# A chunked-attention and expert-routing kernel: first loads by casting DMA, routing matmuls placed later, another order of the last chain

## The chip, the cores and the metric

The kernel runs on one core of one Trainium2 chip. The metric is the device time of one execution in microseconds (us). The time before is the median of three runs, 166.93 us (166.66 to 167.89). A profile is of another single execution: its span, from the first to the last instruction, is 161.9 us, and that execution's time 163.59 us.

The engines are named as in the profile: PE (TensorE; its weight loads are PEld), DVE (VectorE), ACT (ScalarE), POOL (GpSimd), SP (SyncE). [...]

## The reference

Two layers, one after the other. Attention in chunks of 32 queries, each over 8 memory rows, 16 rows to the left, the chunk and 8 rows to the right; batch 4, 8 heads, 768 positions, head size 64:

```python
for c in range(nc):                              # nc = 768 // 32
    k_ctx = k[:, :, l_start:r_end]               # up to 56 rows
    k_full = np.concatenate([mem_k, k_ctx], axis=2)
    v_full = np.concatenate([mem_v, v_ctx], axis=2)
    scores = scale * np.matmul(q_c, k_full.transpose(0, 1, 3, 2))
    a = np.exp(scores - max); a = a / (sum + 1e-09)
    out[:, :, c_start:c_end] = np.matmul(a, v_full)
```

Then, for each batch, a gate score for each of the 768 rows x of 512 numbers; the 128 rows with the highest score go through a feed-forward net (FFN, 512 to 1024 to 512), and its output, weighted by the sigmoid of the score, is added to the row:

```python
scores = np.einsum('bsd,d->bs', x, w_gate)
for b in range(B):
    top_idx = np.argpartition(-scores[b], capacity)[:capacity]    # capacity = 128
    xe = x[b, top_idx]
    ye = np.maximum(xe @ w1, 0.0) @ w2
    g = 1.0 / (1.0 + np.exp(-scores[b, top_idx]))
    out[b, top_idx] = x[b, top_idx] + g[:, None] * ye
```

## The kernel before

The attention takes two heads (a pair) at a time: 4 pairs in a batch, 16 in all (n = 0 to 15). In each, q, k and v are transposed by PE, the scores are formed in two halves, exponentiated by ACT into `es`, and multiplied with v. The loads for two pairs (`load_unit`) are one DMA for each of k, q, v and cast fp32 to fp16 on the way; only the very first pair is loaded as fp32 and cast by DVE and ACT.

```python
def load_unit(u):
    for src, dst, nm in ((k, k16s, "k16"), (q, q16s, "q16"), (v, v16s, "v16")):
        t = ld.tile([96, 4, 512], F16, tag=nm, ...)
        dst[2 * u], dst[2 * u + 1] = t[:, 0:2, :], t[:, 2:4, :]
        if u:  nc.gpsimd.dma_start(out=t, in_=head_ap(src, 2 * u, 4))
        else:  nc.gpsimd.dma_start(out=dst[1], in_=head_ap(src, 1, 2))
for src, nm, eng in ((k, "k", nc.sync), (q, "q", nc.scalar), (v, "v", nc.sync)):
    first[nm] = cst.tile([96, 2, 512], FP, ...)
    eng.dma_start(out=first[nm], in_=head_ap(src, 0, 2))
# ... cut: constants, memory rows, units 1 to 3
```

`fill(n)` issues n matmuls of zeros (128x512) whose result nobody uses; they keep PE occupied. Before the loop:

```python
nc.vector.tensor_copy(out=k16s[0], in_=first["k"])
nc.scalar.copy(out=q16s[0], in_=first["q"])
nc.vector.tensor_copy(out=v16s[0], in_=first["v"])
fill(11); tr_k(0); tr_q(0); fill(4)
mem_rows(memk16, memkT); mem_cols(kws[0], memkT, 0)
fill(3); tr_v(0); scores(0, 0)
mem_rows(memv16, memvT)
for n in range(3): mem_cols(vws[n], memvT, n)
fill(4); tr_k(1); fill(4); scores(0, 1); tr_q(1)
fill(3); back_v(0); tr_v(1); fill(2)
late_constants()
```

The loop works ahead: pass n forms the scores of pair n+1, the values of pair n, and transposes pair n+2. Between its stages stand eight hooks, numbered i to i+7, into which the routing of an earlier batch is put:

```python
for n in range(NPR):                     # NPR = 16
    b, pr = divmod(n, NP); i = 8 * n
    nf = 0 if n in (2 * NP, 3 * NP) else 1
    if b >= 1 and pr == 0: m_store(b - 1)        # writes the batch's x to HBM
    # ... cut: at n == 14, m_alloc(LAST), m_x16(LAST, first half)
    scores(n + 1, 0, nf if b == 0 else 0); hook(i)
    tr_q(n + 2);                           hook(i + 1)
    values(n, 0, nf);                      hook(i + 2)
    tr_k(n + 2);                           hook(i + 3)
    scores(n + 1, 1, nf);                  hook(i + 4)
    back_v(n + 1)
    # ... cut: at n == 14, m_dot(LAST, first half of the columns, scrA)
    hook(i + 5)
    values(n, 1, nf);                      hook(i + 6)
    tr_v(n + 2);                           hook(i + 7)
    # ... cut: load_unit, load_w
```

The routing of batch b begins at hook 32(b+1). Its steps and their places (`at(place, step)`):

```python
dots, cmps, counts = (0, 3, 6, 7, 8, 11), (15, 16, 19, 22, 23, 24), (17, 18, 20, 23, 24, 25)
row0, row1, gate, sel, fetch = 9, 13, 14, 26, 29
# b == LAST - 1: dots (0,1,3,4,6,7), cmps (11,12,14,15,16,17), counts (12,14,15,16,17,18),
#                row0, row1, gate, sel, fetch = 7, 9, 13, 19, 20
# m_dot:   DVE, gate score of 128 rows           -> scr
# m_row:   PE transposes of scr (fp32), ACT copy -> brow (all scores on every partition)
# m_cmp:   DVE, brow < scr                       -> gr
# m_count: PE, 6 matmuls gr x ones               -> p_c (how many score higher)
# m_mask:  DVE, count < 128, running sum         -> mask, incl
# m_slot:  PE, 1 matmul; DVE                     -> slot
# m_sel:   DVE, 6 comparisons with iota          -> sel
# m_fetch: PE sel x aux -> DVE idx, gate; POOL gathers the rows xe from HBM by idx
if b < LAST - 1:
    at(33, m_rows)        # PE transposes xe, ACT copy -> xeT
    at(35, m_ffn1, 0)     # PE 16 matmuls, ACT ReLU -> hT
    at(37, m_ffn1, 1)
    at(39, m_ffn2)        # PE 8 matmuls, ACT -> y; POOL adds y to the rows in HBM
```

All these steps of batches 0 to 2 share one PSUM buffer, `pmm` (tile p_m, p_e, p_f in the profile); those of the last batch use the two buffers of the scores (p_l). After the loop:

```python
b = LAST
m_store(b)
m_dot(b, range(NB), 2, 4, scrB)
nc.vector.tensor_tensor(out=mods[b].scr, in0=scrA, in1=scrB, op=ALU.add)
fill(4)
m_row(b, 0, 4); m_gate_exp(b); m_row(b, 4, 6, "dve")
m_rows(b - 1); fill(3)
m_cmp(b, range(NB)); m_x16(b, 0, 6, 2, 4)
m_ffn1(b - 1, 0); m_count(b, range(0, 3))
m_ffn1(b - 1, 1); m_count(b, range(3, 6))
m_mask(b); m_slot(b); m_ffn2(b - 1)
m_sel(b); m_gate(b); m_gather(b); m_aux(b)
m_ffn1(b, 0); m_ffn1(b, 1); m_ffn2(b)
```

Of the kernel before, what the change touches and what calls it, by code (L numbers as in the profile page):

```python
# [17 lines left out]
def _dap(x, offset, dims):  # L18
    return bass.AP(tensor=x.tensor, offset=offset, ap=[list(d) for d in dims])
# [7 lines left out]
def kernel(  # L27
# [13 lines left out]
    nc = tc.nc  # L41
# [32 lines left out]
    def head_ap(src, n, heads):  # L74
        b, pr = divmod(n, NP)
        return _dap(src, (b * H + 2 * pr) * HD, [[512, 96], [HD, heads], [1, 512]])

    def load_unit(u):
        for src, dst, nm in ((k, k16s, "k16"), (q, q16s, "q16"), (v, v16s, "v16")):
            t = ld.tile([96, 4, 512], F16, tag=nm, name=f"{nm}_{u}")  # L80
            dst[2 * u], dst[2 * u + 1] = t[:, 0:2, :], t[:, 2:4, :]
            if u:
                nc.gpsimd.dma_start(out=t, in_=head_ap(src, 2 * u, 4))
            else:
                nc.gpsimd.dma_start(out=dst[1], in_=head_ap(src, 1, 2))


    first = {}
    for src, nm, eng in ((k, "k", nc.sync), (q, "q", nc.scalar), (v, "v", nc.sync)):
        first[nm] = cst.tile([96, 2, 512], FP, tag=f"{nm}f", name=f"{nm}f")  # L90
        eng.dma_start(out=first[nm], in_=head_ap(src, 0, 2))


    prow = cst.tile([128, 1], I32, tag="prow")
    nc.gpsimd.iota(prow, pattern=[[0, 1]], base=0, channel_multiplier=1)
    memk16 = cst.tile([B * H, n_mem * D], F16, tag="memk16")
    memv16 = cst.tile([B * H, n_mem * D], F16, tag="memv16")
    nc.gpsimd.dma_start(out=memk16, in_=_dap(mem_k, 0, [[n_mem * D, B * H], [1, n_mem * D]]))
    ident16 = cst.tile([128, 128], F16, tag="ident16")
    nc.gpsimd.memset(ident16, 1.0)  # L100
    nc.gpsimd.affine_select(out=ident16, in_=ident16, pattern=[[1, 128]], compare_op=ALU.is_equal, fill=0.0,
                            base=0, channel_multiplier=-1)
    nc.gpsimd.dma_start(out=memv16, in_=_dap(mem_v, 0, [[n_mem * D, B * H], [1, n_mem * D]]))
    for u in range(4):
        load_unit(u)


# [9 lines left out]
    def fill(n):  # L117
        fill_into(pmm.tile([128, 1, 512], FP, tag="pm", name="p_f")[:, 0, :], n)
# [3 lines left out]
    nc.vector.memset(pads[:, :, 0:1], 0.0)  # L122
    nc.vector.memset(pads[:, :, 49:50], 0.0)
    wgb = cst.tile([128, Dm], FP, tag="wgb")
    nc.sync.dma_start(out=wgb, in_=_dap(moe_w_gate, 0, [[0, 128], [1, Dm]]))

    pi = cst.tile([128, 1], I32, tag="pi")
    nc.vector.tensor_scalar(out=pi, in0=prow, scalar1=15, scalar2=None, op0=ALU.bitwise_and)
# [24 lines left out]
        vws.append(cst.tile([128, NG, 128], F16, tag=f"vw{i}", name=f"vw{i}"))  # L153
        nc.vector.tensor_copy(out=vcs[i][:, :, :, 64], in_=ones8[:, :].unsqueeze(2).to_broadcast([128, NG, 2]))

    memkT = cst.tile([128, NPR, n_mem], F16, tag="memkT")
    memvT = cst.tile([128, NPR, n_mem], F16, tag="memvT")

    def mem_rows(src, dst):
        p_mk = pmm.tile([128, n_mem, B * H], F16, tag="pm", name="p_mk")  # L160
        for j in range(n_mem):
            for hh in range(2):
                nc.tensor.transpose(out=p_mk[64 * hh:64 * hh + 64, j, :], in_=src[:, D * j:D * j + D],
                                    identity=ident16[0:B * H, 0:B * H])
        for hh in range(2):
            nc.vector.tensor_copy(out=dst[64 * hh:64 * hh + 64, :, :].rearrange("p n j -> p j n"),  # L166
                                  in_=p_mk[64 * hh:64 * hh + 64, :, hh::2])


# [43 lines left out]
    def tr_q(n):  # L213
        if n >= NPR:
            return
        p_q = pvv.tile([128, 8, 128], F16, tag="pv", name="p_q")[:, :, 0:96]
        transposes(q16s, n, p_q)
        qT = att.tile([128, 96, 8], F16, tag="qT", name="qT")
        nc.scalar.copy(out=qT, in_=p_q.rearrange("p j t -> p t j"))  # L219
        qTs[n] = qT  # L220

    def mem_cols(t, src, n):
        eng = nc.vector if n < 4 else nc.gpsimd
        eng.tensor_copy(out=t.rearrange("p g (j t) -> p g j t", t=16)[:, :, :, 15],  # L224
                              in_=src[:, n:n + 1, :].to_broadcast([128, NG, n_mem]))

    def tr_k(n):
        if n >= NPR:
            return
        transposes(k16s, n)  # L230
        kw = kws[n % SLOTS]
        nc.vector.tensor_copy(out=kw.rearrange("p g (j t) -> p g j t", t=16),  # L232
                              in_=_sap(p_t, 0, [[12, NG], [100, 8], [1, 16]]))
        if n:
            mem_cols(kw, memkT, n)

    def tr_v(n):
        if n >= NPR:
            return
        transposes(v16s, n)  # L240
        vw = vws[n % SLOTS]
        nc.scalar.copy(out=vw.rearrange("p g (j t) -> p g j t", t=16)[:, :, :, 0:15],  # L242
                       in_=_sap(p_t, 0, [[12, NG], [100, 8], [1, 15]]))
# [71 lines left out]
    def m_store(b):  # L315
        x = xs[b]
        nc.sync.dma_start(out=_dap(out, b * S * Dm, [[Dm, 96], [96 * Dm, NB], [1, Dm]]), in_=x[0:96, :, :])
        nc.sync.dma_start(out=_dap(out, (b * S + 576) * Dm, [[Dm, 32], [32 * Dm, NB], [1, Dm]]), in_=x[96:128, :, :])
# [17 lines left out]
    def m_x16(b, lo, hi, pr0=0, pr1=NP):  # L336
        c0, c1 = 2 * D * pr0, 2 * D * pr1
        nc.scalar.copy(out=mods[b].x16[:, lo:hi, c0:c1], in_=xs[b][:, lo:hi, c0:c1])
# [128 lines left out]
    def moe_steps(b):  # L467

        st = {}

        def at(i, f, *a):
            st.setdefault(i, []).append(lambda: f(b, *a))

        at(0, m_alloc)
        dots, cmps, counts = (0, 3, 6, 7, 8, 11), (15, 16, 19, 22, 23, 24), (17, 18, 20, 23, 24, 25)
        row0, row1, gate, sel, fetch = 9, 13, 14, 26, 29
        if b == LAST - 1:
            dots, cmps, counts = (0, 1, 3, 4, 6, 7), (11, 12, 14, 15, 16, 17), (12, 14, 15, 16, 17, 18)
            row0, row1, gate, sel, fetch = 7, 9, 13, 19, 20
        for i in range(NB):  # L480
            at(dots[i], m_dot, (i,))
        at(row0, m_row, 0, 4)
        at(row1, m_row, 4, 6)
        at(row1, m_gate_exp)
        at(gate, m_gate)
        for i in range(NB):
            at(cmps[i], m_cmp, (i,))
        for i in range(NB):
            at(counts[i], m_count, (i,))
        at(counts[NB - 1], m_mask)  # L490
        at(sel, m_slot)
        at(sel, m_sel)
        at(fetch, m_fetch)
        if b < LAST - 1:
            at(33, m_rows)
            at(35, m_ffn1, 0)
            at(37, m_ffn1, 1)
            at(39, m_ffn2)
        return st


# [6 lines left out]
        for f in places.get(i, ()):  # L508
            f()

    nc.vector.tensor_copy(out=k16s[0], in_=first["k"])  # L511
    nc.scalar.copy(out=q16s[0], in_=first["q"])
    nc.vector.tensor_copy(out=v16s[0], in_=first["v"])
    fill(11)
    tr_k(0)
    tr_q(0)
    fill(4)
    mem_rows(memk16, memkT)
    mem_cols(kws[0], memkT, 0)
    fill(3)  # L520
    tr_v(0)
    scores(0, 0)
    mem_rows(memv16, memvT)
    for n in range(3):
        mem_cols(vws[n], memvT, n)
    fill(4)
    tr_k(1)
    fill(4)
    scores(0, 1)
    tr_q(1)  # L530
    fill(3)
    back_v(0)
    tr_v(1)
    fill(2)
    late_constants()
    scrA = mod.tile([128, NB], FP, tag="scrA", name="scrA")
    scrB = mod.tile([128, NB], FP, tag="scrB", name="scrB")
    for n in range(NPR):
        b, pr = divmod(n, NP)
        i = 8 * n  # L540
        nf = 0 if n in (2 * NP, 3 * NP) else 1
        if b >= 1 and pr == 0:
            m_store(b - 1)
        if n == NPR - 2:
            m_alloc(LAST)
            m_x16(LAST, 0, NB, 0, 2)
        scores(n + 1, 0, nf if b == 0 else 0)
        hook(i)
        if 3 <= n + 3 < NPR:
            mem_cols(vws[(n + 3) % SLOTS], memvT, n + 3)  # L550
        tr_q(n + 2)
        hook(i + 1)
        values(n, 0, nf)
        hook(i + 2)
        tr_k(n + 2)
        hook(i + 3)
        scores(n + 1, 1, nf)
        hook(i + 4)
        back_v(n + 1)
        if n == NPR - 2:  # L560
            m_dot(LAST, range(NB), 0, 2, scrA)
        hook(i + 5)
        values(n, 1, nf)
        hook(i + 6)
        tr_v(n + 2)
        hook(i + 7)
        if n % 2 == 1 and n // 2 + 4 < NPR // 2:
            load_unit(n // 2 + 4)
        if n in (0, 2, 4, 6):
            load_w(n)  # L570
            load_w(n + 1)
# [3 lines left out]
    m_store(b)  # L575
    m_dot(b, range(NB), 2, 4, scrB)
    nc.vector.tensor_tensor(out=mods[b].scr, in0=scrA, in1=scrB, op=ALU.add)
    fill(4)
    m_row(b, 0, 4)
    m_gate_exp(b)  # L580
    m_row(b, 4, 6, "dve")
    m_rows(b - 1)
    fill(3)
    m_cmp(b, range(NB))
    m_x16(b, 0, 6, 2, 4)
    m_ffn1(b - 1, 0)
    m_count(b, range(0, 3))
    m_ffn1(b - 1, 1)
    m_count(b, range(3, 6))
    m_mask(b)  # L590
    m_slot(b)
    m_ffn2(b - 1)
    m_sel(b)
    m_gate(b)
    m_gather(b)
# [39 lines left out]
```

## Time and profile before

| | busy us | share of the span |
|---|---|---|
| PE matmuls | 131.6 | 81% |
| PE weight loads | 94.3 | 58% |
| DVE | 91.8 | 57% |
| ACT | 82.2 | 51% |
| POOL | 47.2 | 29% |
| granted PE clock, mean | 0.801 | |
| DMA, mean | 127 GB/s | |

The page has a busy row for each engine over 40 slices of the span, with the granted PE clock (PEclk) and the DMA beside them in tenths. Waits are put down to the instruction or DMA that ended them; "p_m L381 <- DVE gr L371" reads: a matmul of line 381 waited for DVE's result gr of line 371. In the whole span such waits of PE come to 6.4 us for gr, 3.2 us for the gathered rows xe, and 1.5 and 1.6 us for the copied memory rows.

### The profile page before, as it was taken

The numbers are of one execution on the slowest core, as the hardware profiler recorded it, in microseconds if no ns is written. First come the engines' busy times: TensorE is split into PE (matmuls) and PEld (weight loads), VectorE is DVE, ScalarE is ACT, GpSimd is POOL, SyncE is SP. The second block draws the span as 40 slices with busy tenths as digits, with TensorE's granted clock in tenths as the row PEclk, the third lists the DMA queues.
The fourth block names the chain that finished last, engine by engine and source line by source line (L and its number), as shares of the span: only waits on it lengthen the run. The fifth ranks groups of instructions, "written<-read, shape, count | busy, mean of one in ns | idle before, by whom it ended". The sixth has DMA issues, their size and how long they took to land. (4 is left out here: it accounts for less than half of the span.)

```text
span 161.9 us, 4777 instructions
## 1 busy us (share of the span) xinstructions
PE 131.6 (81%) x2047; PEld 94.3 (58%) x2047; DVE 91.8 (57%) x282; ACT 82.2 (51%) x160; POOL 47.2 (29%) x79
## 2 busy tenths in 40 slices
PE   6866989999999788969997889959876798688900
PEld 2332457777776666758775667848465573476500
DVE  5455227755897855835658575736469579555000
ACT  3314267898886627261777533465586220543310
POOL 7886142013675250182052200402230020002130
PEclk9995699999999955555999655687999555599996
DMA  4999999998799999059993000194050022910532
GB/s 150 249 205 207 205 206 209 205 187 140 73 217 290 253 207 200 12 111 223 247 146 59 0 4 0 11 285 135 0 65 4 0 34 71 280 42 0 69 29 36
DMA packets 15781, 20.49 MB, mean 127 GB/s; under 512 B 848, under 2 KB 10960, under 8 KB 15760
## 3 DMA queue, kind: packets, MB, share of 16 engines
q0 software_dynamic: 11792, 12.45, 49.1%
q1 hardware_dynamic: 3760, 7.34, 15.3%
q10 hardware_dynamic: 208, 0.39, 0.8%
q8 instruction: 16, 0.26, 0.6%
q14 instruction: 5, 0.04, 0.1%
HBM read 24.25 MB, written 7.34 MB: 195 GB/s over the span
## 5 line engine op out<-in xcount | busy, mean ns | idle before, releaser
L271 ACT ACTIVATE es<-p_s,maskb 128x256 f16<-128x256 f32 x96 | 38.5, 474 | 20.5 <-PE p_s L266 20.4
L292 PEld LDWEIGHTS <-es 128*32 128x32 f16 (+1 forms) x384 | 25.3, 127 | 5.6 <-issue 2.2
L292 PE MATMUL p_w<-vc,es 128*32 128x65 f16 (+1 forms) x384 | 27.2, 220 | 0.0
L242 ACT COPY vw<-p_t 128x960 f16<-128x960 f16 x16 | 15.4, 961 | 20.8 <-PE p_t L210 20.8
L224 POOL COPY kw<-memkT 128x64 f16<-128x64 f16 x12 | 8.4, 703 | 54.0 <-DVE kw L232 54.0
L295 DVE RECIPROCAL rd<-p_w 128x6 f32<-128x6 f32 x32 | 6.2, 195 | 29.1 <-PE p_w L292 28.7
L115 PE MATMUL p_f<-zeros 128*128 128x512 f16 x38 | 14.7, 535 | 5.1 <-DVE memvT L166 1.6
L296 DVE TENSOR_TENSOR x<-p_w,rd 128x384 f32<-128x384 f32 x32 | 17.8, 557 | 1.1
L251 DVE COPY vc<-p_v 128x1024 f16<-128x1024 f16 x16 | 11.1, 691 | 9.9 <-PE p_v L250 9.7
L333 DVE SCALAR_TENSOR_TENSOR junk<-x,wgb 128x512 f32<-128x512 f32 (+1 forms) x30 | 16.2, 581 | 0.0
L464 POOL DMA_INDIRECT out_dram<-y,idx x4 | 6.5, 1617 | 33.1 <-ACT y L463 27.3
L115 PEld LDWEIGHTS <-zeros 128*128 128x128 f16 x83 | 8.8, 114 | 12.4 <-issue 5.2
L371 DVE TENSOR_SCALAR gr<-brow,scr 128x768 f16<-128x768 f32 x24 | 13.7, 622 | 0.1
L219 ACT COPY qT<-p_q 128x768 f16<-128x768 f16 x16 | 13.0, 813 | 0.6 <-PE p_q L210 0.6
L115 PE MATMUL p_w<-zeros 128*128 128x512 f16 x28 | 12.9, 462 | 0.0
L266 PE MATMUL p_s<-qT,kw 64*128 64x96 f16 x256 | 12.7, 228 | 0.0
L250 PE MATMUL p_v<-ident,vw 128*128 128x128 f16 x128 | 11.9, 247 | 1.0 <-ACT qT L219 1.0
L232 DVE COPY kw<-p_t 128x1024 f16<-128x1024 f16 x16 | 11.0, 685 | 2.6 <-PE p_t L210 2.2
L266 PEld LDWEIGHTS <-kw 64*128 64x128 f16 x256 | 7.4, 104 | 7.3 <-issue 6.3
L381 PE MATMUL p_m<-onec,gr 128*128 128x1 f16 x108 | 5.6, 167 | 6.4 <-DVE gr L371 6.4
L210 PE MATMUL p_t<-ident,k 96*64 96x96 f16 x256 | 10.1, 232 | 0.7 <-DVE k L511 0.7
L250 PEld LDWEIGHTS <-vw 128*128 128x128 f16 x128 | 9.0, 110 | 2.4 <-issue 1.2
(114 smaller groups left out, 185.0 us busy)
## 6 DMA issues: line engine op xcount, KB each, us to landing
out_dram<-x SPq DMA_DIRECT2D x4, 1152.0 KB, 7.7
k<-in_k_dram POOLq DMA_DIRECT2D x7, 384.0 KB, 11.2
q<-in_q_dram POOLq DMA_DIRECT2D x7, 384.0 KB, 12.4
v<-in_v_dram POOLq DMA_DIRECT2D x7, 384.0 KB, 13.4
w_sb<-in_moe_w_dram POOLq DMA_DIRECT2D x8, 256.0 KB, 9.6
out_dram<-x SPq DMA_DIRECT2D x4, 384.0 KB, 9.1
qf<-in_q_dram ACTq DMA_DIRECT2D x1, 384.0 KB, 5.1
kf<-in_k_dram SPq DMA_DIRECT2D x1, 384.0 KB, 4.7
```

Source lines behind the costliest of these rows:

```text
L115: nc.tensor.matmul(out=ap, lhsT=zeros[:, 0:128], rhs=zeros, start=True, stop=True)
L219: nc.scalar.copy(out=qT, in_=p_q.rearrange("p j t -> p t j"))
L232: nc.vector.tensor_copy(out=kw.rearrange("p g (j t) -> p g j t", t=16), in_=_sap(p_t, 0, [[12, NG], [100, 8], [1, 16]]))
L242: nc.scalar.copy(out=vw.rearrange("p g (j t) -> p g j t", t=16)[:, :, :, 0:15], in_=_sap(p_t, 0, [[12, NG], [100, 8], [1, 15]]))
L250: nc.tensor.transpose(out=p_v[:, g, :, :], in_=vws[n % SLOTS][:, g, :], identity=ident16)
L251: nc.vector.tensor_copy(out=vcs[n % SLOTS][:, :, :, 0:64], in_=p_v)
L266: nc.tensor.matmul(out=p_s[:, h, 96 * gi:96 * gi + 96], lhsT=kw[o:o + 64, g, :], rhs=qf[o:o + 64, 96 * g:96 * g + 96], start=True, stop=True)
L271: nc.scalar.activation(out=es[:, :, :, 32 * c:32 * c + 32], in_=pv[:, :, :, 32 * c:32 * c + 32], func=AF.Exp, bias=maskb[:, c:c + 1], scal ...
L292: nc.tensor.matmul(out=p_x[r0:r1, i, h, :], lhsT=es[:, h, gi, q0:q1], rhs=vc[:, GROUPS[half][gi], h, 0:65], start=True, stop=True)
L296: nc.vector.tensor_tensor(out=xs[b].rearrange("p g (n h d) -> p n g h d", n=NP, d=D)[:, pr, 3 * half:3 * half + 3], in0=p_x[:, :, :, 0:64] ...
L333: nc.vector.scalar_tensor_tensor(out=junk[:, c0:c1], in0=x[:, bl, c0:c1], scalar=1.0, in1=wgb[:, c0:c1], op0=ALU.mult, op1=ALU.mult, accum ...
L371: nc.vector.tensor_scalar(out=m.gr[:, bl, :], in0=m.brow, scalar1=m.scr[:, bl:bl + 1], scalar2=None, op0=ALU.is_lt)
```

## The change

It does four things. The first pair's k, q and v are loaded by the casting DMA of POOL too, in the order in which they are needed, so that the casts on DVE and ACT and the fp32 buffers go; the load of the gate weights stands in pass 1. The transposed memory rows are stored in the order in which PE leaves them, so their copy writes without a stride. The routing steps get other places: those of PE stand at least two hooks behind the vector work that they need, and the FFN of batches 0 and 1 comes later. And in the last chain the rows of batch 2 and both halves of its first FFN layer stand ahead of the last batch's row transposes, the counts are one block, and some fills move. Core of the diff (cuts marked):

```diff
+    def load_half(src, dst, n):
+        nc.gpsimd.dma_start(out=dst[n], in_=head_ap(src, n, 2))
+    load_unit(0)            # now only allocates
+    load_half(k, k16s, 0)
     nc.gpsimd.iota(prow, ...)
-    # first[nm]: fp32 loads on sync and scalar, casts on DVE and ACT
+    load_half(q, q16s, 0)
+    # ... cut: ident16, load of memk16
+    load_half(v, v16s, 0)
+    # ... cut: load of memv16
+    for src, dst in ((k, k16s), (q, q16s), (v, v16s)):
+        load_half(src, dst, 1)
-    nc.sync.dma_start(out=wgb, in_=...w_gate...)     # at the start
+        if n == 1:                                    # in the loop
+            nc.sync.dma_start(out=wgb, in_=...w_gate...)
-    memkT = cst.tile([128, NPR, n_mem], ...)          # memvT alike
+    memkT = cst.tile([128, n_mem, NPR], ...)
-        nc.vector.tensor_copy(out=dst[...].rearrange("p n j -> p j n"), in_=p_mk[..., hh::2])
+        nc.vector.tensor_copy(out=dst[...], in_=p_mk[..., hh::2])
```

```diff
+        p = dict(dots=(0, 3, 6, 7, 8, 11), row0=12, row1=15, gate=17, cmps=(18, 19, 22, 23, 24, 27),
+                 counts=(22, 23, 26, 27, 28, 31), mask=32, slot=34, sel=35, fetch=38, rows=45, ffn=(47, 49, 51))
+        if b == LAST - 2:
+            p.update(fetch=37, rows=43, ffn=(45, 46, 47))
         if b == LAST - 1:
+            p = dict(dots=(0, 1, 3, 4, 6, 7), row0=9, row1=11, gate=12, cmps=(13, 14, 15, 17, 18, 19),
+                     counts=(16, 17, 18, 20, 21, 22), mask=22, slot=24, sel=24, fetch=26)
```

```diff
-    fill(11)
+    fill(8)
     tr_k(0)
+    fill(2)
     tr_q(0)
-    fill(4)
     # ... cut: likewise 3 -> 2, 0 -> 1, 4 -> 0, 4 -> 2, 3 -> 2, 2 -> 1
-        nf = 0 if n in (2 * NP, 3 * NP) else 1
+        nf = 1
     # ... cut: at n == 14 m_x16(LAST) after the second half of the scores; scrA's m_dot from n == 14 to n == 15
-    fill(4)
+    m_rows(b - 1)
+    m_ffn1(b - 1, 0)
+    m_ffn1(b - 1, 1)
     m_row(b, 0, 4)
     m_gate_exp(b)
     m_row(b, 4, 6, "dve")
-    m_rows(b - 1)
-    fill(3)
     m_cmp(b, range(NB))
+    m_ffn2(b - 1)
     m_x16(b, 0, 6, 2, 4)
-    m_ffn1(b - 1, 0)
-    m_count(b, range(0, 3))
-    m_ffn1(b - 1, 1)
-    m_count(b, range(3, 6))
+    m_count(b, range(NB))
     m_mask(b)
     m_slot(b)
-    m_ffn2(b - 1)
+    fill(3)
     m_sel(b)
```

## The prediction

> **What bounds the kernel now.** I read the page's slices first, then busy time by stage, then TensorE's (PE's) timeline inside the stages where the clock is low. Two rows of the slices (40 slices of 4.05 us) belong side by side:
>
> ```profile
> PE   6866989999999788969997889959876798688900
> PEclk9995699999999955555999655687999555599996
> ```
>
> PE is busy nearly everywhere, yet in 16 slices it was granted under 0.7 of its clock. Cut at the main loop's borders (a pass of the loop starts with the scores of the next pair of heads), the stages are: start, passes 0 to 4, passes 5 to 11, passes 12 and 13, and the rest.
>
> ```profile
> core 0: us, PE busy (x) PEld busy (x) DVE busy (x) ACT busy (x) POOL busy (x), PEclk, DMA share, GB/s
> 0.00:22.54 22.54, 16.57 (x184) 7.88 (x184) 10.08 (x41) 7.62 (x13) 13.39 (x32) 0.85 1.08 203
> 22.54:46.23 23.69, 23.51 (x500) 17.77 (x498) 15.40 (x41) 19.50 (x40) 8.35 (x16) 1.00 1.05 167
> 46.23:104.37 58.14, 51.68 (x840) 39.74 (x836) 37.08 (x105) 32.16 (x66) 17.54 (x27) 0.71 0.66 132
> 104.37:124.46 20.09, 15.35 (x268) 11.85 (x266) 12.14 (x33) 12.71 (x25) 3.71 (x4) 0.92 0.42 100
> 124.46:161.90 37.44, 24.51 (x270) 17.09 (x267) 17.06 (x70) 10.17 (x18) 4.17 (x3) 0.73 0.29 61
> ```
>
> Columns: stage, length, busy time per engine, granted clock, DMA share, GB/s. Passes 0 to 4 are the healthy state: 4.74 us each, PE full, clock 1.00. Passes 5 to 11 are PE-bound too (51.68 of 58.14 us) but at clock 0.71. Why it falls is in PE's timeline (start, length, group, idle before it and its releaser):
>
> ```profile
> 87.86 0.18 PE L378 MATMUL p_m<-zero,ltri 128*128 128x6 f16 x1
> 88.86 0.30 PE L381 MATMUL p_m<-onec,gr 128*128 128x1 f16 x6 [0.82 <-DVE gr L371]
> 89.03 0.38 PE L115 MATMUL p_w<-zeros 128*128 128x512 f16 x1
> ...
> 107.02 0.40 PE L417 MATMUL p_e<-ident,xe 128*128 128x128 f16 x4 [1.85 <-DMA xe<-out_dram,idx]
> ```
>
> PE stands in order at a routing matmul whose comparison VectorE (DVE) has just begun. Soon after each such gap the same 16 transposes take 0.85 us instead of 0.53. Asked in 1 us steps, the clock falls near 56.5, 90.6, 107.7 and 124.7 and returns near 76.9, 104.3, 111.1 and 141.8: all about whole multiples of 3.41 us apart. The gaps just before the falls are 0.88, 0.82, 1.85 and 1.27 us; gaps of 0.32 to 0.36 us made no fall, and one of 0.84 made none either. Once low, the clock returned after a stretch with PE dense throughout, mostly in the FFN.
>
> At the start PE waits for the fp32 loads, a cast, and a copy of the memory rows; at the end a chain runs through the gate scores, comparisons, counts and selection of the last batch:
>
> ```profile
> 5.51 0.90 DVE L511 CAST k<-kf 96x1024 f16<-96x1024 f32 x1 [1.97 <-DMA kf<-in_k_dram]
> ...
> 9.08 1.45 DVE L166 COPY memkT<-p_mk 64x128 f16<-64x128 f16 x2 [0.43 <-PE p_mk L163]
> ...
> 10.60 0.82 PE L115 MATMUL p_f<-zeros 128*128 128x512 f16 x3 [1.55 <-DVE memkT L166]
> ...
> 137.92 0.17 DVE L577 TENSOR_TENSOR scr<-scrA,scrB 128x6 f32<-128x6 f32 x1
> ...
> 140.32 3.27 DVE L371 TENSOR_SCALAR gr<-brow,scr 128x768 f16<-128x768 f32 x6
> ...
> 146.31 1.07 DVE L403 TENSOR_SCALAR sel<-iota,slot 128x128 f16<-128x128 f16 x6
> ```
>
> [...] the gather here takes 3.4 to 3.7 us to landing, and I use that.
>
> **Part 1: the start.** Removed: the casts (DVE 0.90 and 0.69 us, ScalarE/ACT 1.05), of which the k cast lies on the path: k arrives at 5.51, PE starts at 6.47. In place of 384 KB fp32 loads there are 192 KB fp16 landings, first in POOL's stream, issued near 0.8 us. The slices show about 205 GB/s for casting loads: 192 KB is 1.0 us. Taking 3.5 us of latency from the gather, k lands at 0.8+3.5+1.0 = 5.3, q at 6.3, v (behind a small one) near 7.5. So PE starts about 1.1 us earlier. Also, each copy of the transposed memory rows took 720 ns writing with a stride; with plain writes I put it at 0.25 to 0.3 (a 128x64 copy takes 0.30). Four copies save 1.7 us, and PE waited for them (1.5+1.6 us). Before, there were 31 fills up to the loop, now 18; 13 fewer at 0.22 to 0.43 us are 3 to 5 us of PE, part of which only filled waits. Stepping through the new order with measured durations (tr_k 5.4, memkT ready 8.6, tr_v 9.2, scores 10.2, tr_k(1) 11.1, kw(1) ready 13.2, tr_q(1) 13.2, qT 15.0, back_v 15.1, tr_v(1) 15.7) the loop starts near 16.4 instead of 22.54: **-6.1 us**. One catch: "the gate weights later" holds in program order only. SyncE has nothing ahead of that load and no wait, so it goes out at 0.8 us instead of 1.74[...]; its 256 KB at some 200 GB/s are about 1 us that may come on top of the 5.3.
>
> **Part 2: passes 5 to 11.** Passes 0 to 4 stay 23.7 us. One batch of routing and FFN costs PE, at full clock: rows 0.65+0.43, counts 6x0.22, ffn1 2x0.95, ffn2 1.85, other 0.5: 6.8 us. A pass without it is 4.67. Two batches over seven passes, with all but about one count stage: 7x4.67+2x6.8 = 46.3 less what falls into pass 12 (about 1): 45.3 ideal. Each count now stands four hooks, some 2.3 us, behind its comparison, so I expect those waits gone. DVE needs per pass 2x0.76+0.69+0.69 = 2.9 us, plus 0.65 per dot, 0.57 per comparison, 1.07 for the selection. It runs late in pass 8 (mask, slot, selection, four dots: 7.3 us in a 5 us pass) and PE loses about 1 us in passes 8 and 9. New waits appear in pass 9: the gathered rows leave their index at the DVE late (5 us after the hook's place in a clean pass, +3.7 us DMA), a gap of about 1.2; then row and FFN matmuls share the single PSUM buffer p_m, and the second row stage waits for the FFN's ReLU, about 0.8. Stepping through gives 5.2, 5.2, 5.4, 5.2, 9.0, 8.2, 5.4 = 43.8 us, and I add 2.5 for one short fall of the clock in pass 9, ended by the FFN: 46.3 against 58.14, **-11.8 us**.
>
> **Part 3: passes 12 and 13.** Pass 12 gives DVE mask, slot, selection and six dots on top of its own 2.9: 0.35+0.23+1.07+3.9+2.9 = 8.5 us where PE has 5. PE waits about 1.6 for the selection, and the index goes out only near 7.2 us after the pass starts, so rows of batch 1 come at 10.9, a gap of some 1.7. That drops the clock; the row, both ffn1 halves and ffn2 then share p_m. I get 23 us against 20.09: **+2.9**.
>
> **Part 4: from pass 14 on.** Pass 14: 3.2 us plus 1.35 of counts, 5 with waits, end of counts tc. Then slot and selection to tc+2.1, six half dots to 4.2, one value product, then index at 5.3, gather landed 9.0; second product, six more half dots, the gate scores scr ready at 8.4. But PE's order now puts the rows and both ffn1 halves of batch 2 ahead of the row transposes of batch 3. At half clock (PE idle from 3.3 to 9.0) that is 0.63+0.7+1.89+0.6+1.89: transposes begin at 14.7 although scr is ready at 8.4. Then 1.5, row copies 1.0, six comparisons 3.3, counts' tail, mask and slot 1.2: selection at 21.7. Selection to end took 161.9-146.3 = 15.6, kept: end at tc+37.3. So 5+37.3 = 42.3 against 37.44: **+4.9**.
>
> **Sum.** -6.1-11.8+2.9+4.9 = -10.1 us, span about 151.8. The times lie 5.0 above the profiled span (166.93 against 161.9); kept, 156.8. I say **157.0 us**.
>
> **Rivals.** (a) The clock stays high through the whole loop because passes 12 and 13 fill better than I think (a fill in pass 12 is new). Passes 0 to 4 show it can: then 20 us for them and no fall in pass 9, and 150 us timed. Against it: DVE's 8.5 us in pass 12. (b) The clock falls earlier, at small DVE waits of 0.2 to 0.4 us in passes 6 to 9, and stays low until an FFN, which comes later now than before (hook 47 instead of 35):[...] 165 to 167, no gain but the start's.[...] against: waits of 0.36 kept the clock. (c) First loads as slow as the old second ones (5.8 to 6.5 us to landing): k at 6.6, the start gives 4.5: 158.5. (d) The old tail order was better and costs more than +4.9, say +7: 159.
>
> **Range and chances.** Start -4 to -7.5, passes 5 to 11 -4 to -15, passes 12 and 13 -1 to +5, tail +1 to +7; their joint spread is about 5 us each way: 150 to 163. 2% under 166.93 is 163.6. Faster 0.86, same 0.10, slower 0.04.
>
> **What would show it.** Loop start near 16.4 and no cast of k, q, v; waits of the counting matmuls for gr gone in batches 0 and 1; clock 1.00 through passes 5 to 8; a gap of over 1 us at the rows of pass 9 and in pass 12; the row transposes of the last batch behind ffn1, waiting for nothing of their own. Wrong it would be made by a clock that falls in passes 5 to 8 without waits, by a first k landing after 7, or by gathered rows that arrive early enough for the tail's new order to hide ffn1.

## The result and the profile after

The changed kernel takes 161.32 us (median of four, 159.29 to 165.07) against 167.41 us (166.66 to 167.91) for the kernel before in the same series. The ratio is 0.954, with a 95% interval of 0.946 to 0.963. Ratios here leave out executions more than 1.5% above the fastest of their kernel (so 0.954 is not the quotient of the two medians, 0.964); where too few were left, only the median and its range are given.

The profiled execution took 159.29 us, its span is 157.6 us (before: 163.59 and 161.9), and the mean granted clock is 0.851 instead of 0.801. The slices of the page after, PE's busy tenths and its granted clock (3.94 us a slice):

```profile
PE   6789999999999999901989999949875006877900
PEclk9955699999999999985559999999998555599975
```

The low patch of slices 15 to 19 of before (passes 6 to 8) is gone; PE's nines reach from slice 4 to slice 17. Two holes stand there that before had not: PE busy 0 and 1 in slices 18 and 19, and 0 and 0 in slices 32 and 33. With each the clock is low: 0.50 from 69.5 to 83.2 us and from 120.7 to 137.8. Cut at the same borders of the main loop as before, with the same columns (stage, length, busy time per engine, clock, DMA share, GB/s):

```profile
0.00:18.03 18.03, 14.82 (x171) 7.49 (x171) 7.49 (x39) 6.63 (x12) 13.59 (x32) 0.72 0.97 154
18.03:41.87 23.84, 23.66 (x500) 17.77 (x499) 15.06 (x36) 19.55 (x40) 9.71 (x19) 0.99 1.21 209
41.87:94.28 52.41, 43.56 (x834) 34.16 (x830) 35.08 (x94) 31.99 (x67) 18.07 (x26) 0.87 0.72 150
94.28:111.95 17.67, 14.91 (x258) 11.03 (x256) 13.49 (x44) 11.38 (x23) 1.91 (x3) 1.00 0.38 99
111.95:157.60 45.65, 22.61 (x283) 16.84 (x282) 16.63 (x69) 11.33 (x19) 6.02 (x4) 0.75 0.27 55
```

| stage | before | after | difference | predicted |
|---|---|---|---|---|
| start | 22.54 | 18.03 | -4.5 | -6.1 |
| passes 0 to 4 | 23.69 | 23.84 | +0.2 | 0 |
| passes 5 to 11 | 58.14 | 52.41 | -5.7 | -11.8 |
| passes 12, 13 | 20.09 | 17.67 | -2.4 | +2.9 |
| from pass 14 | 37.44 | 45.65 | +8.2 | +4.9 |
| span | 161.9 | 157.6 | -4.3 | -10.1 |

The two holes are waits for gathered rows. PE's timeline after (start, length, group, the idle time before it and its releaser):

```profile
5.84 0.53 PE L210 MATMUL p_t<-ident,k 96*64 96x96 f16 x16 [1.01 <-DMA k<-in_k_dram]
...
74.42 0.61 PE L417 MATMUL p_e<-ident,xe 128*128 128x128 f16 x4 [7.59 <-DMA xe<-out_dram,idx]
...
104.25 0.40 PE L417 MATMUL p_e<-ident,xe 128*128 128x128 f16 x4 [1.46 <-DMA xe<-out_dram,idx]
...
117.69 0.18 PE L394 MATMUL p_m<-incl,ltri 128*128 128x1 f16 x1 [0.92 <-DVE incl L389]
...
130.51 0.61 PE L417 MATMUL p_e<-ident,xe 128*128 128x128 f16 x4 [10.26 <-DMA xe<-out_dram,idx]
131.79 1.87 PE L451 MATMUL p_m<-xeT,w_sb 128*128 128x128 f16 x16 [0.67 <-ACT xeT L419]
134.34 1.86 PE L451 MATMUL p_m<-xeT,w_sb 128*128 128x128 f16 x16 [0.68 <-ACT hT L453]
136.00 1.49 PE L344 MATMUL p_l<-ident,scr 128*128 128x128 f32 x6
```

The counting matmuls (L381) of batches 0 and 1 no longer wait for gr in passes 5 to 11. PE now waits at the rows of batch 0 (7.59 us in pass 9) and of batch 2 (10.26 us in the last chain). Passes 5 to 8 take 5.3, 5.2, 5.2 and 4.9 us at clock 1.00; pass 9 alone takes 17.8, pass 10 8.8.

Why the rows come so late is in the queues, as the experiments show. Over the span, the time from a gather's issue to its landing was at least / in the middle / at most 3.4/3.7/3.7 us before, and after:

```profile
DMA to landing us min/median/max: 3.5/8.1/10.3
```

POOL's timeline, first of the kernel before, then of the kernel after, where the gather and the last loads of k, q and v (384 KB each as written) are issued:

```profile
68.84 1.05 POOL L410 DMA_INDIRECT xe<-out_dram,idx  x1 [0.74 <-DVE gate L441]
69.88 0.74 POOL L83 DMA_DIRECT2D k<-in_k_dram  x1
```

```profile
56.80 0.69 POOL L83 DMA_DIRECT2D k<-in_k_dram  x1
57.48 0.68 POOL L83 DMA_DIRECT2D q<-in_q_dram  x1
58.14 0.68 POOL L83 DMA_DIRECT2D v<-in_v_dram  x1
...
64.10 1.30 POOL L410 DMA_INDIRECT xe<-out_dram,idx  x1 [2.79 <-DVE gate L441]
...
122.35 0.99 POOL L410 DMA_INDIRECT xe<-out_dram,idx  x1 [7.70 <-DVE rd L295]
```

Before, the gather of batch 0 stood ahead of the last loads (hook 61, in pass 7, which ends with them). Moved by nine hooks to 70, it stands behind 1152 KB of them in the same queue. And SyncE's queue, after, has a store of 1536 KB under way in both places: the one of batch 1 goes out 6 us before the gather of batch 0 (its two parts landed 11.2 and 13.0 us after their issue), the last one half a microsecond after the gather of batch 2 (7.1 and 8.0 us):

```profile
58.02 0.32 SPq L317 DMA_DIRECT2D out_dram<-x  x1
...
122.87 0.32 SPq L317 DMA_DIRECT2D out_dram<-x  x1
```

### The profile page after: what moved, and what is told of

It reads as the page before. It is cut to its first block, busy times and chain, and to the rows that moved or that the text cites. A ratio compares the mean times of both kernels' runs of the same rounds, so it can differ in the third digit from the quotient of the medians.

```text
span 157.6 us, 4751 instructions
## 1 busy us (share of the span) xinstructions
PE 119.6 (76%) x2036; PEld 87.3 (55%) x2036; DVE 87.8 (56%) x280; ACT 80.9 (51%) x159; POOL 49.3 (31%) x82
## 5 line engine op out<-in xcount | busy, mean ns | idle before, releaser
L292 PEld LDWEIGHTS <-es 128*32 128x32 f16 (+1 forms) x384 | 21.7, 112 | 4.5 <-issue 0.2
L292 PE MATMUL p_w<-vc,es 128*32 128x65 f16 (+1 forms) x384 | 23.0, 203 | 0.0
L296 DVE TENSOR_TENSOR x<-p_w,rd 128x384 f32<-128x384 f32 x32 | 17.8, 558 | 1.1
L417 PE MATMUL p_e<-ident,xe 128*128 128x128 f16 x12 | 1.6, 278 | 19.3 <-DMA xe<-out_dram,idx 19.3
L419 ACT COPY xeT<-p_e 128x512 f16<-128x512 f16 x3 | 1.8, 585 | 22.5 <-PE p_e L417 22.5
L116 PE MATMUL p_w<-zeros 128*128 128x512 f16 x32 | 12.5, 391 | 0.2 <-DVE idx L439 0.2
L417 PEld LDWEIGHTS <-xe 128*128 128x128 f16 x12 | 0.9, 120 | 19.7 <-DMA xe<-out_dram,idx 19.7
L451 PEld LDWEIGHTS <-w_sb 128*128 128x128 f16 x128 | 10.4, 122 | 2.6 <-issue 1.7
L266 PE MATMUL p_s<-qT,kw 64*128 64x96 f16 x256 | 11.6, 212 | 0.0
L266 PEld LDWEIGHTS <-kw 64*128 64x128 f16 x256 | 6.7, 97 | 7.7 <-issue 6.6
L116 PE MATMUL p_f<-zeros 128*128 128x512 f16 x21 | 9.3, 563 | 2.0 <-DVE zeros L110 1.3
L250 PE MATMUL p_v<-ident,vw 128*128 128x128 f16 x128 | 10.2, 225 | 0.6 <-ACT qT L219 0.6
## 6 DMA issues: line engine op xcount, KB each, us to landing
w_sb<-in_moe_w_dram POOLq DMA_DIRECT2D x8, 256.0 KB, 11.9
```

Source lines behind the costliest of these rows:

```text
L116: nc.tensor.matmul(out=ap, lhsT=zeros[:, 0:128], rhs=zeros, start=True, stop=True)
L266: nc.tensor.matmul(out=p_s[:, h, 96 * gi:96 * gi + 96], lhsT=kw[o:o + 64, g, :], rhs=qf[o:o + 64, 96 * g:96 * g + 96], start=True, stop=True)
L292: nc.tensor.matmul(out=p_x[r0:r1, i, h, :], lhsT=es[:, h, gi, q0:q1], rhs=vc[:, GROUPS[half][gi], h, 0:65], start=True, stop=True)
L296: nc.vector.tensor_tensor(out=xs[b].rearrange("p g (n h d) -> p n g h d", n=NP, d=D)[:, pr, 3 * half:3 * half + 3], in0=p_x[:, :, :, 0:64] ...
L451: nc.tensor.matmul(out=p_h[:, 0, 128 * fi:128 * fi + 128], lhsT=w1_sb[:, dch, f0:f0 + 128], rhs=m.xeT[:, dch, :], start=(dch == 0), stop=( ...
```

## The experiments

The theory from this profile: the change itself does what it was made for, and most of the gain that was predicted and did not come is lost at two late gathers, each caused by what stands near it in the queues. Rivals: the start alone brings the gain, and the places bring none; the rows are late because DVE delivers the index late, not because of the transfers; the tail costs because the row transposes stand behind the first FFN layer, not because of the gather; the clock's fall behind each wait is the loss, not the wait.

Twelve kernels ran. Each is compared with the kernel before on its own chip (medians 164.9 to 167.4). "Tail" is read from each profile: from the end of batch 2's counts (the start of the idle time before its mask's matmul, L394) to the end of the span. It leaves out everything that happened earlier. Pass 9 is given where the new places make it comparable.

| kernel | us, median (range) | ratio to before, 95% | pass 9 | tail |
|---|---|---|---|---|
| before | 167.4 (of the first series) | 1 | | 34.7 |
| after | 161.32 (159.29 to 165.07) | 0.954 [0.946, 0.963] | 17.8 | 40.8 |
| before + start | 161.26 (158.61 to 162.65) | 0.974 [0.949, 0.998] | | 35.1 |
| before + places | 156.46 (151.92 to 156.62) | | 15.7 | 35.8 |
| before + new last part | 164.81 (162.86 to 164.83) | 1.004 [0.990, 1.018] | | 34.7 |
| after, old last part | 154.51 (152.32 to 156.50) | | 17.4 | 35.1 |
| after, old order of the chain | 158.62 (155.92 to 162.73) | 0.952 [0.942, 0.962] | 16.1 | 38.6 |
| after, index ahead of the dots | 153.37 (152.63 to 155.28) | 0.931 [0.923, 0.939] | 17.8 | 34.2 |
| after, loads behind the gather | 155.36 (151.01 to 156.31) | | 11.6 | 42.7 |
| after, store behind the gather | 155.47 (154.50 to 156.70) | 0.946 [0.937, 0.954] | 12.5 | 41.1 |
| after, gate weights from ACT | 160.84 (158.70 to 163.12) | 0.970 [0.958, 0.983] | 18.5 | 41.1 |
| after, fills in the wait | 159.33 (156.48 to 160.85) | 0.953 [0.944, 0.962] | 15.5 | 40.9 |
| after, loads and index | 148.59 (145.70 to 152.13) | 0.891 [0.878, 0.905] | 9.0 | 35.9 |
| after, loads, store, index, transposes | 142.70 (141.85 to 145.65) | 0.865 [0.857, 0.873] | 9.0 | 33.6 |

### The parts alone

Three kernels take one part of the diff each. "Start": first loads, order of the memory rows, gate weights, fills ahead of the loop. "Places": the table of hooks and `nf = 1`. "New last part": the two moved groups of pass 14 and 15 and everything after the loop.

> The kernel before with the start alone changed (casting loads of the first pair, copies of the memory rows without stride, fewer fills). If the parts simply add up: the loop starts near 18.0 us as in the changed kernel, 4.5 us earlier than before, all later stages keep their lengths, and the time falls by 4 to 5 us, to about 162.5. Rival: [...]the time may move by 2 to 4 us more either way, with the same waits in the trace.

> The kernel before with the other places of the routing steps alone (and the fill in passes 8 and 12). From the changed kernel's stages: passes 5 to 8 at full clock, no wait for gr; passes 5 to 11 52 to 53 us instead of 58, passes 12 and 13 17.7 instead of 20; the wait for the gathered rows in pass 9 about 7 us, as in the changed kernel, because the gather now stands behind the loads of the last unit. The old tail behind it: the gather of batch 2 comes later than before but the row transposes of the last batch do not wait for it; 0 to +3. Time 159 to 162. Rival (the wait in pass 9 comes from the changed start): the wait would be under 2 us here and the time near 153.

> The kernel before with the other order of the last chain alone. The index of batch 2 is computed early here (place 19 and 20), so its rows arrive near 134 and the feed-forward of batch 2 fits ahead of the row transposes: the tail moves by -1 to +1.5, time 166 to 169. If instead the new order is bad in itself, the row transposes stand some 5 us behind their scores as well, and the time is 170 or more.

The start alone has the wide ratio 0.949 to 0.998. In its profiled execution the same 16 transposes took PE 0.85 us instead of 0.53 up to 26 us (below, under what was unexpected), so the second pass began at 27.40 against 27.61 before: no gain in that one, while another of its executions was 4 us shorter. The places alone, at 156.5 us, beat the whole change: passes 5 to 8 take 5.3, 5.2, 5.2 and 5.0 us, and the late gather is there too, so it comes with the places and not with the start. The 156.5 us are less than the 159 to 162 that were expected. PE's timeline in it:

```profile
78.29 0.61 PE L417 MATMUL p_e<-ident,xe 128*128 128x128 f16 x4 [6.00 <-DMA xe<-out_dram,idx]
```

The new last part alone costs nothing that can be measured: 1.004, and a tail of 34.7 us as before. So it is not the start alone that brings the gain. But the parts do not add: with gains of about 6 us (start; 4 by its ratio) and 11 us (places) and 0 for the last part one would expect 150 to 152 us, and the whole change takes 161.

### The last chain: what makes it dear only together

The old last part put back into the changed kernel, scrA's half dots and the first x16 copies (ACT's casts of the rows to fp16) of pass 14 included:

```diff
-        if n == NPR - 1: m_dot(LAST, range(NB), 0, 2, scrA)    # pass 15, behind hook(i)
+        if n == NPR - 2: m_dot(LAST, range(NB), 0, 2, scrA)    # pass 14, ahead of hook(i + 5)
     # ... cut: m_x16 of pass 14; after the loop, all lines of the last diff undone
```

> The changed kernel with the whole last part as before (order of the last chain and place of the six half dots scrA in pass 14); start and places stay changed. The parts alone gave about -6 (start), -11 (places) and -3 or nothing (tail), together far more than the -6 of the whole change. Theory (the new tail is harmless in the old loop, where batch 2's rows come early, and harmful behind the new places, where the index of batch 2 waits for the half dots and its gather runs beside the last store): start and places add up, 150 to 153, and the row transposes wait for their scores alone. Rival (start and places disturb each other[...]): 156 or more.

Only the order after the loop put back, the half dots left in pass 15:

```diff
-    m_rows(b - 1); m_ffn1(b - 1, 0); m_ffn1(b - 1, 1)
+    fill(4)
     m_row(b, 0, 4); m_gate_exp(b); m_row(b, 4, 6, "dve")
+    m_rows(b - 1); fill(3)
     m_cmp(b, range(NB))
     # ... cut: ffn1, counts and ffn2 interleaved as before
```

> The changed kernel with the last chain in the old order (row transposes of the last batch ahead of rows and feed-forward of batch 2, counts in two halves between them). The row transposes run at 125.2, as soon as scr is there, instead of 136.0; but the rows of batch 2 still arrive only near 130.5 and stand ahead of the counts, so the selection comes near 138 instead of 142.6: -3.5 to -5.5 us. Rival (the comparisons and not the matmul order set the chain): -9 to -11, as much as the transposes come earlier.

And the new order kept, with the half dots moved behind the place of batch 2's index, two hooks later:

```diff
         hook(i)
-        if n == NPR - 1: m_dot(LAST, range(NB), 0, 2, scrA)
     # ... cut: tr_q, hook(i + 1), first values, hook(i + 2) with m_fetch
+        if n == NPR - 1: m_dot(LAST, range(NB), 0, 2, scrA)
```

> The changed kernel with the six half dots of the last batch (scrA) placed behind the index of batch 2 in VectorE's order (pass 15, after hook 2). The index comes 2.1 us earlier (119.9 instead of 122.0), so the gather is issued ahead of the last store. Theory[...]: it lands in 3.5 to 4 us, near 123.7 instead of 130.5, and the time falls by 5 to 7 us. Rival (only the late index counts, as in the prediction): the rows come 2.1 us earlier and the time falls by about 2.

The last one takes 6.6 us off the tail (40.8 to 34.2) and the ratio from 0.954 to 0.931, intervals apart. POOL's and then PE's timeline in it:

```profile
120.35 1.00 POOL L410 DMA_INDIRECT xe<-out_dram,idx  x1 [5.95 <-DVE gate L441]
```

```profile
123.71 0.61 PE L417 MATMUL p_e<-ident,xe 128*128 128x128 f16 x4 [3.37 <-DMA xe<-out_dram,idx]
```

The index is 2.0 us earlier (the share of the late index), the rows 6.8 us: the other 4.8 are the landing, 3.3 to 3.5 us instead of 8.1, with the gather issued 2.6 us ahead of the last store and no longer 0.5. With the old last part the gather is no earlier than in the kernel after, but 1.4 us ahead of its store; POOL's, SyncE's and PE's timelines there:

```profile
122.97 0.99 POOL L410 DMA_INDIRECT xe<-out_dram,idx  x1 [7.90 <-DVE gate L441]
```

```profile
124.38 0.32 SPq L317 DMA_DIRECT2D out_dram<-x  x1
```

```profile
126.68 1.54 PE L344 MATMUL p_l<-ident,scr 128*128 128x128 f32 x6 [1.33 <-DVE scr L578]
128.01 0.63 PE L417 MATMUL p_e<-ident,xe 128*128 128x128 f16 x4
```

It landed within 3.8 us, during the transposes, and the rows wait for nothing: a tail of 35.1 us. The half dots (pass 14 here) stand ahead of the index in this kernel too; what differs from after is the lead on the store and the order behind it. Its 154.5 us lie between the 150 to 153 expected and the rival's 156. The old order alone, half dots still ahead of the index, gains 2.2 us of tail (38.6), less than the 3.5 to 5.5 expected: the transposes then go at 123.96 but the rows still wait, 4.42 us. The order of the transposes is about a third of the 6.1 us by which the tail grew. In total time the old order alone is not to be told from the change (0.952 and 0.954).

So the last part is harmless with the old places, where the index stands in pass 14, ahead of the half dots, and dear with the new ones, where `fetch=26` puts it in pass 15 behind them. The cost belongs to the pair.

### The gather of batch 0: queue or store

The last loads moved behind the gather's place:

```diff
+        if n == 8: load_unit(7)                    # behind hook(i + 6)
-        if n % 2 == 1 and n // 2 + 4 < NPR // 2:   # behind hook(i + 7)
+        if n in (1, 3, 5):
             load_unit(n // 2 + 4)
```

> The changed kernel with the loads of the last unit issued after the gather of batch 0 (in pass 8) instead of before it. Theory (queue order): the gather waited in the one software queue behind these loads; it now lands 4 to 5 us after its issue instead of 10.3, PE's wait in pass 9 falls from 7.6 to under 2 us, the low clock behind it from 13.7 us to 3.4 to 7, and the time by 7 to 9 us, to about 153. Rival (the store of batch 1 that runs beside it takes the bandwidth): the gather still takes 7 us or more and the time falls by less than 3 us. Rival (index late on VectorE): no change.

The store of batch 1 issued later, by ACT in pass 9:

```diff
-        if b >= 1 and pr == 0: m_store(b - 1)
+        if b in (1, 3) and pr == 0: m_store(b - 1)
     # ... cut
+        if n == 9: m_store(1, nc.scalar)           # behind hook(i + 5)
```

> The changed kernel with the store of batch 1 issued from ScalarE in pass 9, after the gathered rows were used, instead of at 58 us. Loads of the last unit stay ahead of the gather. Bandwidth rival:[...] the gather lands near 68.5 to 69.5 instead of 74.4, PE's wait in pass 9 falls from 7.6 to 2 or 3 us, time -5 to -8. If queue order alone counted and the store did not matter, the wait would stay at 6 us or more and the time within 2 us.

PE's timeline at these rows: loads away, store away, and both away (the last kernel below):

```profile
68.83 0.40 PE L417 MATMUL p_e<-ident,xe 128*128 128x128 f16 x4 [2.16 <-DMA xe<-out_dram,idx]
```

```profile
69.78 0.40 PE L418 MATMUL p_e<-ident,xe 128*128 128x128 f16 x4 [3.20 <-DMA xe<-out_dram,idx]
```

```profile
68.16 0.40 PE L418 MATMUL p_e<-ident,xe 128*128 128x128 f16 x4 [0.94 <-DMA xe<-out_dram,idx]
```

Issue to landing of this gather was 10.3 us in the kernel after, 4.8 with the loads away, 5.9 with the store away, and 3.6 at most with both away; PE's wait for the rows 7.59, 2.16, 3.20 and 0.94 us; pass 9 17.8, 11.6, 12.5 and 9.0 us. The index is not what was late: in after and in the last kernel alike the gather is issued 1.6 us into pass 9. Both loads and store matter, and neither alone explains it: the loads are in the gather's own queue, the store in another. Six other kernels with both in the way had 8.7 to 11.0 us, so the steps are larger than the spread. How the time is shared between the two queues, no view shows. In the kernel with loads moved and index ahead of the dots, the same gather landed within 3.8 us though the store stood as in the 4.8 case. So about 1 us of these landings is not explained by the order of issue, and the store delays the gather mainly together with the loads: by 4.4 us with them, by about 0 to 1.2 us without.

### The clock behind the wait

Thirty fills (128x512) put into the wait of pass 9, ahead of hook(i + 5), to keep PE busy while the rows come:

```diff
+        if n == 9: fill(30)
         hook(i + 5)
```

> The changed kernel with 30 matmuls of zeros put into PE's wait for the gathered rows in pass 9 (30 x 0.216 = 6.5 us, inside the 7.6 us wait, so they should delay nothing). The wait stays, only the clock is kept. If the low clock behind the wait (13.7 us) is what costs beside the wait itself: no fall in passes 9 and 10, pass 9 13 to 14 us instead of 17.8, pass 10 about 7.6 to 8.2, time -4 to -6. Rival (passes 9 and 10 are bound by the shared PSUM buffer and ScalarE, not by PE's clock): under 2 us.

PE's timeline in it:

```profile
68.88 6.63 PE L116 MATMUL p_f<-zeros 128*128 128x512 f16 x30 [0.81 <-ACT brow L350]
75.58 0.38 PE L417 MATMUL p_e<-ident,xe 128*128 128x128 f16 x4
```

The wait is filled, and no fall of the clock follows (16 transposes take 0.53 us at 76.65): pass 9 15.5 us and pass 10 7.6 us, 3.5 us less for the two than after. The rows are used 11.9 us into pass 9 in both kernels, so that is the part of the fall; the wait itself, 6.65 us more than with the fast gather, is the larger one. The clock's fall is about a third of the 10 us that passes 9 and 10 lose against the last kernel below (26.6 and 16.5). The total is not to be told from after (0.953 and 0.954): in this profile the clock fell at 103.1 instead, and pass 13 took 13.3 us for 12.0. For the wait in the last chain no run tells the wait and the fall apart.

### The gate weights

The prediction saw that the load "later" would go out at once, since SyncE waits for nothing: it was issued at 0.82 us, earlier than before (1.74). Issued by ACT in pass 1 (at 23.24 us), it really is later:

```diff
         if n == 1:
-            nc.sync.dma_start(out=wgb, in_=...)
+            nc.scalar.dma_start(out=wgb, in_=...)
```

> The changed kernel with the gate weights loaded really late: issued from ScalarE in pass 1, behind its work, instead of at 0.8 us from SyncE, which has nothing ahead of it. Theory[...]: first transposes of k at 5.0 to 5.5 instead of 5.84, loop start 0.3 to 0.8 us earlier, time -0.3 to -1. Rival (the latency of the first software DMA sets it): k at 5.8, no change.

k's first transposes start at 5.06 us, 0.8 us earlier than after, but nine other kernels with the gate weights at 0.82 us had them at 5.3 to 5.4: the edit is worth about 0.3 us there. The loop's first scores stand at 15.62, 2.9 us earlier than after. Most of that is not the edit either: two kernels without it have them at 15.9, and in all three the clock did not fall at 8.1 us, as it did after (16 transposes take 0.53 us there from 6.9 on, and 0.85 in after at 16.84), but only behind 18.8. And the time stays the same (160.84). PE's timeline says where it went:

```profile
17.54 0.53 PE L210 MATMUL p_q<-ident,q 96*64 96x96 f16 x16 [1.57 <-DMA q<-in_q_dram]
```

The first pass needs q of pair 2, which lands no sooner, and the clock falls behind that wait of 1.57 us (19.7, for 3.4 us): the second pass starts at 23.45, against 23.25 after. The gain of a faster start ends at the second unit's loads.

### The remedies together

Loads behind the gather and index ahead of the half dots:

> The changed kernel with the loads of the last unit behind the gather of batch 0 and the half dots scrA behind the index of batch 2, that is the two single edits together. They concern two waits far apart (passes 9 and 15), so they should add: -6 and -8 from 161.3, 146 to 149. Rival (the clock falls elsewhere once these waits are gone): 151 or more.

And with the late store as well, and the last batch's row transposes between the rows of batch 2 and their first FFN layer:

```diff
     m_rows(b - 1)
-    m_ffn1(b - 1, 0)
-    m_ffn1(b - 1, 1)
     m_row(b, 0, 4); m_gate_exp(b); m_row(b, 4, 6, "dve")
+    m_ffn1(b - 1, 0)
+    m_ffn1(b - 1, 1)
     m_cmp(b, range(NB))
```

> The changed kernel with both of those edits, the store of batch 1 issued after the gathered rows of batch 0 were used, and the row transposes of the last batch placed between the rows and the feed-forward of batch 2. The gather of batch 0 then runs alone: 3.5 us, PE's wait in pass 9 under 1.5 us. The row transposes run near the time at which scr is there instead of 4 us later, of which 2 to 3 us stay because the counts still stand behind the feed-forward. 142 to 146. Rival (low clock in the tail takes it): no faster than the kernel with two edits.

148.6 us and 142.7 us: 0.891 and 0.865 of the kernel before. The last beats both kernels by a wide margin. Its slices:

```profile
PE   6776599999999999999789999948986438888600
PEclk9999968999999999999999999999999755899965
```

No slice of the loop is empty; the clock falls at 19.0 us for 3.4 and then not until 111.2, in the last chain; all three gathers land in 3.5 to 3.6 us, and PE waits for them 0.94, 1.64 and 3.54 us.

## Why the prediction was right, and where it failed

The 157.0 us were 4.3 below the measured median, and the range of 150 to 163 held it; the direction was right. That the sum came out so near is luck: its terms for passes 5 to 11 and for passes 12 and 13 were off by 6.1 and 5.3 us with opposite signs. Two small sums in it are wrong as well (the seven steps of passes 5 to 11 add up to 43.6 and not 43.8, the routing of a batch to 6.65 and not 6.8); neither matters here.

**Part 1, the start (-6.1 against -4.5): direction right, size off.** The memory-row copies take 0.30 us each, as put. k was used at 5.84 in this execution instead of 5.3; nine other kernels with the same first loads had it at 5.3 to 5.4, so that term was good and rival c's 6.6 wrong. Its parts hit by luck: the load goes out at 1.41 us, not at 0.8, and lands within 4.0 us in those nine, where 4.5 was put. The mis-sized terms are two. The stepping ran at full clock, while the clock was at half from 8.1 to 18.3. And where it was not (three kernels with first scores at 15.6 to 15.9, near the 16.4 predicted) the first pass took 7.7 to 7.9 us: it waited 1.5 to 1.7 for q, and the clock fell behind that (at 19.0 to 19.7). The prediction took "passes 0 to 4 stay 23.7 us" from a kernel whose loop started late enough for its loads. The second pass starts at 23.0 to 23.8 in these three and in four of the other eight, against 27.61 before: about 4 us is what the start is worth in them, by either way. In the other four it starts at 24.5 to 27.4, in three of them behind the slow start told at the end.

**Part 2, passes 5 to 11 (-11.8 against -5.7): mechanism right, one step wrong.** Passes 5 to 8 were put at 5.2, 5.2, 5.4, 5.2 and took 5.3, 5.2, 5.2, 4.9; the counting waits are gone and the clock stays at 1.00, so rival b falls. The wait of the second row stage for the ReLU was 0.69 where 0.8 was put. What failed is "+3.7 us DMA": the gather took 10.3, so the "gap of about 1.2" was 7.59, and the "one short fall" of 2.5 us was 13.7 us at half clock. Pass 9 took 17.8 us instead of 9.0. With the gather at 3.6 us it took the 9.0, and pass 10 7.6. The duration was read in a kernel where the gather stood ahead of the loads; the prediction kept it for the new place (hook 70 instead of 61) and did not ask what was now in the queue before it.

**Part 3, passes 12 and 13 (+2.9 against -2.4): wrong sign.** The wait for the selection was 0.22 us, not 1.6. DVE was as full as put (busy 5.62 of the 5.70 us of pass 12), but the sum counted all six dots against the selection, and only two of them stand ahead of it in DVE's order; two follow it and two run in pass 13. DVE's timeline after:

```profile
95.28 0.69 DVE L333 SCALAR_TENSOR_TENSOR junk<-x,wgb 128x512 f32<-128x512 f32 x1
...
97.43 1.14 DVE L403 TENSOR_SCALAR sel<-iota,slot 128x128 f16<-128x128 f16 x6
98.50 0.68 DVE L333 SCALAR_TENSOR_TENSOR junk<-x,wgb 128x512 f32<-128x512 f32 x1
```

The wait for the rows was 1.46, near the 1.7 predicted, but the clock did not fall behind it (1.00 over the stage). That is rival a, in this stage only. In three other kernels with the same instructions here it did fall, and pass 13 took 13.3, 14.7 and 15.1 us instead of 12.0, so after's 12.0 is in part luck too.

**Part 4, from pass 14 on (+4.9 against +8.2): mechanism right, size off.** Counts end 4.8 us after the stage's start (5 predicted), scr is ready 8.3 us later (8.4), and the row transposes stand behind rows and both ffn1 halves, as put. But the rows come at 13.7 after the counts' end, not at 9.0, so everything behind shifts: transposes at 19.2 instead of 14.7, selection at 25.9 instead of 21.7. From there to the end, 15.0 against 15.6. The mis-sized term is again the landing of the gather, 8.1 instead of 3.7 us. Rival d named the order as the cost; the order is 2.2 of the 6 us.

**The offset** of 5.0 us between span and median was 3.7.

## What to carry to other kernels

A DMA's latency read in a profile belongs to its place in the queue; here a gather of at most 3.7 us took 10.3 behind 1152 KB of loads and beside a store, and 3.6 with both away. When a step that ends in a small, urgent transfer is moved, look what bulk transfers now stand ahead of it on the same queue and run beside it on others, and issue the bulk ones after it. Two reorderings that are each free can be dear together; here one moved an index behind a pass border and the other moved vector work to just ahead of it. And a gain at the start ends at the next transfer that was hidden only by the old start, here q of pair 2 with a wait of 1.5 to 1.7 us.

## What was unexpected of the hardware

**A half-speed start that the clock column does not show.** In the profile of the start alone, the window 16 to 20 us (columns as in the stages) and PE's timeline:

```profile
16.00:20.00 4.00, 3.76 (x42) 2.02 (x41) 1.07 (x6) 1.68 (x3) 2.09 (x10) 1.00 1.24 205
```

```profile
17.63 0.85 PE L210 MATMUL p_t<-ident,v 96*64 96x96 f16 x16
...
26.07 0.85 PE L210 MATMUL p_t<-ident,v 96*64 96x96 f16 x16
27.73 0.53 PE L210 MATMUL p_q<-ident,q 96*64 96x96 f16 x16
```

The column says 1.00, but the 16 transposes take 0.85 us up to 26 us and 0.53 from 27.7 on. Two fills in a row take 1.04 us there and one 0.61, so the second adds 0.43; elsewhere it is 0.60, 0.38 and 0.22. The same is seen in four other profiles, with the last slow transposes at 5.1, 14.6, 19.8 and 26.1 us and no fall recorded before; in the rest the early transposes take 0.53. My estimate is that it is worth up to 4 us an execution (the second pass at 27.40 against 23.0 to 23.8), and it may be a good part of why executions of one kernel spread by up to 4.4% (155.92 to 162.73); the durations, not the column, show the state there.

**What drops the clock is still open.** The low stretches of after (from 8.1, 69.5 and 120.7 us) take 10.2, 13.7 and 17.1 us, about 3, 4 and 5 times 3.4, the shortest stretch of before (from 107.7). What makes the clock fall is not settled: the 1.46 and 0.68 us waits of after's pass 13 made no fall, the 1.30 and 0.68 us at the same place in the kernel with the fills did, and in the kernel with the loads moved the clock fell at 93.4 with only some 0.4 us of waits in the 3.4 us ahead of it, a stretch mostly of transposes and routing matmuls. No run was made to tell these apart.

**Half a microsecond of lead is no lead.** A gather issued 0.5 us ahead of a 1536 KB store on another queue landed in 8.0 to 8.7 us in six kernels, after among them. With 1.4 us ahead it landed in at most 3.8, with 2.6 us in 3.3 to 3.5. In the kernel before, the gather at 68.84 (above) landed within 3.7 us although this store followed 1.3 us behind it:

```profile
70.10 0.32 SPq L317 DMA_DIRECT2D out_dram<-x  x1
```

POOL's own instruction for a gather takes 0.99 to 1.30 us in the lines shown, so a lead of 0.5 us ends inside it and one of 1.3 us behind it (1.05 there). That fits; that it is the reason is not shown.
